# Windowed attention and eight experts: slot table from plain one-hots, copies of v a step later, and the second expert's weights on another queue

## The chip, the cores and the metric

The kernel runs on one core of a Trainium2 chip. The core has five engines that run side by side, each with a queue of its own: TensorE (PE: matmuls; the loading of a matmul's stationary operand is listed apart as PEld), VectorE (DVE), ScalarE (ACT), GpSimd (POOL) and SyncE (SP), which here only issues DMA transfers. DMAs are also issued from ScalarE's queue and, with row numbers computed in the kernel, from GpSimd's. The metric is the time of one execution on the device in microseconds. The kernel before took 696.98 us, the median of 3 runs (695.01 to 697.22).

## The reference

Two layers. The first is attention with 8 batches, 8 heads, 576 positions and 64 dimensions; every query sees itself and the 63 keys before it. The second sends each of the 8 x 576 = 4608 tokens (512 numbers each) to one of 8 experts, the one with the largest gate logit, and scales what the expert gives by the gate's probability.

```python
scores = scale * np.matmul(q, k.transpose(0, 1, 3, 2))
mask = (rel >= 0) & (rel < window)          # window = 64
...
attn = attn / (np.sum(attn, axis=-1, keepdims=True) + 1e-09)
return np.matmul(attn, v).astype(np.float32)
...
x = np.ascontiguousarray(attn_out.transpose(0, 2, 1, 3)).reshape(B * S, H * D)
...
logits = x @ w_gate
expert_idx = np.argmax(logits, axis=1)
gate_w = probs[np.arange(N), expert_idx]
perm = np.argsort(expert_idx, kind='stable')
...
    h = np.maximum(x_sorted[lo:hi] @ w1[e], 0.0)      # 512 -> 1024
    y_sorted[lo:hi] = h @ w2[e]                        # 1024 -> 512
return (gate_w[:, None] * y).astype(np.float32)
```

## The kernel before

**Attention.** The work is cut into 16 units (`units`): a batch group of two batches (`bg`, four of them) and a pair of heads (`g`, four of them). A unit has 9 token tiles of 128 tokens, and is worked in three steps of three tiles, so there are 48 steps. One call of `step(s)` issues parts of several steps: the scores of step s+1 (`scored`, L700), their masking and row maximum on VectorE (`masked`, L713), the exponential on ScalarE (`softened`, L723), the turning of step s's probabilities on TensorE with a copy out (`flipped`, L731 and L733), the product of step s-1 with v (`weighted`, L746) and its division (`divided`, L756 to L760), which writes x into a tile of the pool `xsp` (seven tiles, three to a batch group), and the turning of x for the gate's logits (`x_turned`, L771, and `logit`, L783).

The order on each engine is the order in which the code issues (`tc.manual_schedule()`). Two dictionaries, `todo` and `between`, name for each step what is to be issued at its end or in its middle. At every third step, that is once a unit, `load_v(u + 2)` and `load_qk(u + 3)` are issued. v is kept twice, as loaded (`va`) and shifted by half a tile (`vb`); `load_v` issues four DMAs on SP's queue and six GpSimd copies that make `vb` (L638 to L646).

**Routing.** When a batch group's logits are complete (`ripe`), `choose(bg)` finds on VectorE each token's expert and its rank among that expert's tokens. `after` spreads this over the next steps, and with it `weigh` (x times the gate, on GpSimd at L886), `store` (x to DRAM) and `place(j)`. A token's slot is a number; its low part (0 to 127) says the lane, its high part which of 62 columns. `place(j)` writes for token tile j two 128x128 matrices `lo[:, 0, j]` and `lo[:, 1, j]` (L875): the one-hot of the low part, times one of two parts of the token's number (`toks`, from L196 to L199). `slot_table` makes the one-hot of the high part, `hi` (L919), for all 36 token tiles, and multiplies the two for 36 x 2 matmuls that sum into `slots` (`fill`, L927); L937 makes of it the list of token numbers by slot, `perm_i`. `first_tiles` does the same earlier for the first two tiles of expert 0, from the first 27 token tiles alone: `hi_e` has 4 columns, 27 x 2 matmuls at L990, `perm_e` at L993, then `gather_first`.

**Experts.** Tokens are worked in tiles of 256 (two chunks of 128). `hidden(e)` makes the first layer and `output(e)` the second; both use seven products of half-size blocks in place of eight, with sums of weight blocks prepared on GpSimd (`sums_w1`, `sums_w2`, L142) and sums of data on VectorE. `hidden` is a generator of seven parts and `output` of eight, so that the code can issue other work between them: the first tile (`tile0`) is issued in parts among the last batch group's routing, `starts` and the eight parts of `slot_table`. The x of a later tile comes by an indirect DMA (`gather`, L283 and L285), is turned on VectorE in 16 blocks (`turned_blocks`, L324), copied on ScalarE to its place (`keep_turned`, L336) and put into sums (`sums_x`, L342). `some(blocks, n)` issues n of these transposes: in `hidden` 6, 2, 2 and 2 after four of its adds, and `output` issues those that are left. For the second tile, `tile1`, `hidden(0)` is called without blocks, so all 16 are issued in `output`. The result of a tile goes out by `scatter` (L304).

**Memory and weights.** There are two sets of weight buffers. Set 0 exists from the start; set 1 is taken from a pool `wp` that is opened behind the block of the attention and the first two tiles, in memory that pools of that block (`held`) had. Its first loads, w1 and w2 of expert 1, 2 MB each, are issued on SP's queue.

Of the kernel before, what the change touches and what calls it, by code (L numbers as in the profile page):

```python
# [36 lines left out]
def kernel(  # L37
# [130 lines left out]
    lo = consts.tile([P, 2, NJ, P], BF16, name="lo")  # L168
    count = consts.tile([P, E], F32, name="count")
    lane = consts.tile([P, P], BF16, name="lane")  # L170
    low = consts.tile([P, NJ], F32, name="low")
    hi_id = consts.tile([P, NS], BF16, name="hi_id")

    toks = [consts.tile([P, NJ], F32, name=f"tok_{n}") for n in "ab"]
# [5 lines left out]
    with tc.tile_pool(name="tmp", bufs=1) as tmp:  # L180
        iota(e_m[:], pattern=[[1, E]], base=-E, channel_multiplier=0)
        ids = tmp.tile([P, P], F32, name="ids")
        iota(ids[:], pattern=[[1, P]], base=0, channel_multiplier=0)
        V.tensor_copy(out=lane[:], in_=ids[:])
        V.tensor_scalar_add(hi_id[:], ids[:, 0:NS], float(-C))

        tok = tmp.tile([P, NJ], F32, name="tok")
        tok_g = tok[:].rearrange("p (g j) -> p g j", j=NTB)
        for i in range(BG):
            iota(tok_g[:, :, i * NV : (i + 1) * NV], pattern=[[BG * S, NJ // NTB], [P, NV]], base=i * S,  # L190
                 channel_multiplier=1)
            iota(tok_g[i * D : (i + 1) * D, :, BG * NV], pattern=[[BG * S, NJ // NTB]], base=i * S + SM,
                 channel_multiplier=1)
        tok_i = tmp.tile([P, NJ], I32, name="tok_i")
        low_i = tmp.tile([P, NJ], I32, name="low_i")
        V.tensor_scalar(out=tok_i[:], in0=tok[:], scalar1=-1.0, scalar2=float(NT), op0=ALU.mult, op1=ALU.add)  # L196
        V.tensor_single_scalar(low_i[:], tok_i[:], D - 1, op=ALU.bitwise_and)
        V.tensor_copy(out=toks[1][:], in_=low_i[:])
        V.tensor_tensor(out=toks[0][:], in0=tok_i[:], in1=low_i[:], op=ALU.subtract)  # L199
        G.memset(ones[:], 1.0)  # L200
        G.affine_select(
            out=before[:], in_=ones[:], pattern=[[1, P]], compare_op=ALU.is_gt, fill=0.0, base=0,
            channel_multiplier=-1,
        )
        G.memset(keep[:], 1.0)
        G.memset(keep[:, :, 0:1], 0.0)
        V.memset(count[:], 0.0)
# [7 lines left out]
    hi_e = rt.tile([P, NJE, NE * C], BF16, name="hi_e")  # L215
# [129 lines left out]
    def hidden(e, blocks=iter(())):  # L345
# [18 lines left out]
        some(blocks, 6)  # L364
# [6 lines left out]
        some(blocks, 2)  # L371
# [3 lines left out]
        some(blocks, 2)  # L375
# [4 lines left out]
        some(blocks, 2)  # L380
# [186 lines left out]
    with tc.manual_schedule(), ExitStack() as held, ExitStack() as brief:  # L567
        xsp = held.enter_context(tc.tile_pool(name="xsp", bufs=7))
# [63 lines left out]
        def load_v(u, batches=range(BG)):  # L632
            bg, g = units[u]
            va, vb = v_ring[u % NVR]
            for i in batches:
                for h in range(2):
                    nc.sync.dma_start(out=va[:, i, :, h, 0:D], in_=whole(v, u, i, h))
                nc.gpsimd.tensor_copy(  # L638
                    out=vb[0:D, i].rearrange("p j h d -> p (j h d)"),
                    in_=va[D:P, i].rearrange("p j h d -> p (j h d)"),  # L640
                )
                nc.gpsimd.tensor_copy(
                    out=vb[D:P, i, 0 : NV - 1].rearrange("p j h d -> p (j h d)"),
                    in_=va[0:D, i, 1:NV].rearrange("p j h d -> p (j h d)"),
                )
                G.tensor_copy(out=vb[D:P, i, NV - 1, :, 0:D], in_=rests[bg][2][D:P, i, 2 * g : 2 * g + 2])  # L646
# [226 lines left out]
        def place(j):  # L873
            for i in range(2):
                V.tensor_scalar(  # L875
                    out=lo[:, i, j], in0=lane[:], scalar1=low[:, j : j + 1], scalar2=toks[i][:, j : j + 1],
                    op0=ALU.is_equal, op1=ALU.mult,
                )
# [29 lines left out]
        def slot_table(hi):  # L908
# [8 lines left out]
            for n in range(2):  # L917
                js = slice(n * NJ // 2, (n + 1) * NJ // 2)
                V.tensor_tensor(  # L919
                    out=hi[:, js], in0=_inner(at_b[:, js], NS), in1=_ins(hi_id[:], 1, NJ // 2), op=ALU.is_equal  # L920
                )
                yield
            slots = banks[3](0, NS)

            def fill(j):
                for i in range(2):
                    nc.tensor.matmul(slots, lhsT=lo[:, i, j], rhs=hi[:, j], start=(i + j == 0), stop=(i + j == NJ))  # L927

            for j in range(NJE):
                fill(j)  # L930
            for n in range(NST):
                for m in range(ST):
                    place(NJE + n * ST + m)
                yield
            for j in range(NJE, NJ):
                fill(j)
            V.tensor_scalar(out=perm_i[:], in0=slots, scalar1=-1.0, scalar2=float(NT), op0=ALU.mult, op1=ALU.add)  # L937
# [13 lines left out]
        def after(s, routing, bg):  # L951
# [3 lines left out]
            if bg < last - 1:  # L955
# [3 lines left out]
                for m in range(NTB):  # L959
                    do(5 + m * 2 // 3, partial(place, bg * NTB + m))  # L960
                    do(5 + m * 2 // 3, partial(weigh, bg, m, G))
                    if m % ST == ST - 1:
                        do(5 + m * 2 // 3, partial(store, bg, m // ST, G))
# [4 lines left out]
            for m in range(NTB):  # L968
                do(4 + m // 3, partial(place, bg * NTB + m))
# [7 lines left out]
        def first_tiles():  # L977
# [5 lines left out]
                out=hi_e[:], in0=_inner(key[:], NE * C), in1=_ins(hi_id[:, C + 1 : C + 1 + NE * C], 1, NJE),  # L983
                op=ALU.is_equal,
            )
            yield
            slots = banks[next(tr_ring)](0, NE * C)
            for j in range(NJE):
                for i in range(2):
                    nc.tensor.matmul(  # L990
                        slots, lhsT=lo[:, i, j], rhs=hi_e[:, j], start=(i + j == 0), stop=(i + j == NJE)
                    )
            V.tensor_scalar(out=perm_e[:], in0=slots, scalar1=-1.0, scalar2=float(NT), op0=ALU.mult, op1=ALU.add)  # L993
# [4 lines left out]
        V.memset(lo[:, 0, 0:4], 0.0)  # L998
        for _ in range(8):
            nc.tensor.matmul(  # L1000
                banks[7](0, 512), lhsT=lo[:, 0, 0], rhs=lo[:, 0, 0:4].rearrange("p a b -> p (a b)"), start=True,
# [10 lines left out]
        load_v(1)  # L1012
        load_qk(2)
# [12 lines left out]
        def step(s):  # L1026
# [11 lines left out]
            if s >= 0 and s % NST == 0:  # L1038
# [3 lines left out]
                if u + 2 < NU:  # L1042
                    load_v(u + 2)
                if u + 3 < NU:
# [70 lines left out]
        hi = held.enter_context(tc.tile_pool(name="hot", bufs=1)).tile([P, NJ, NS], BF16, name="hi")  # L1115
# [10 lines left out]
        tile1 = chain(hidden(0), output(0, blocks))  # L1126
        for _ in range(8):
            next(tile1)
        regs, end, most = loads()
# [4 lines left out]
    wp = ctx.enter_context(tc.tile_pool(name="wp", bufs=1))  # L1134

    w1s.append(w1_of(wp, 1))
    s1s.append(s1_of(wp, 1))
    w2s.append(w2_of(wp, 1))
    s2s.append(s2_of(wp, 1))


    with tc.manual_schedule():
        load_w1(1)
        load_w2(1)
# [116 lines left out]
```

## Time and profile before

| | |
|---|---|
| runs | 696.98 us median (695.01 to 697.22, 3 runs) |
| the profiled execution | 692.44 us, its span from first to last instruction 690.7 us |
| granted TensorE clock | 0.997 of full speed |
| attention and routing | about 0 to 199 us |
| first tile, with the slot table | about 200 to 231.8 us |
| second tile | 231.8 to 257 us |
| experts 0 (rest) to 7 | 257 us to the end |

All times of instructions are from that one execution, in microseconds from its start. A row of the order of time reads: start, duration of the group, engine, line, operation, what it writes <- what it reads, size, count, and in brackets how long the engine stood idle before it and what ended that. A row of a line's instructions gives the shortest, median and longest duration in ns. Matmuls overlap one another, so a group of them lasts longer than the distance to the next group's start; that distance is the pace. Busy shares are averages over stages with different limits.

### The profile page before, as it was taken

The numbers are of one execution on the slowest core, as the hardware profiler recorded it, in microseconds if no ns is written. First come the engines' busy times: TensorE is split into PE (matmuls) and PEld (weight loads), VectorE is DVE, ScalarE is ACT, GpSimd is POOL, SyncE is SP. The second block draws the span as 40 slices with busy tenths as digits, with TensorE's granted clock in tenths as the row PEclk, the third lists the DMA queues.
The fourth block names the chain that finished last, engine by engine and source line by source line (L and its number), as shares of the span: only waits on it lengthen the run. The fifth ranks groups of instructions, "written<-read, shape, count | busy, mean of one in ns | idle before, by whom it ended". The sixth has DMA issues, their size and how long they took to land. (4 is left out here: it accounts for less than half of the span.)

```text
span 690.7 us, 17952 instructions
## 1 busy us (share of the span) xinstructions
PE 671.8 (97%) x6902; PEld 590.5 (85%) x6902; DVE 500.6 (72%) x1650; ACT 262.2 (38%) x660; POOL 357.0 (52%) x364
## 2 busy tenths in 40 slices
PE   7999999999999999999999999999899999999996
PEld 5888888888788987998899899899599799689995
DVE  5767898898959578775686586577767586866864
ACT  4989888889845011211121121111121121121211
POOL 7316578577771218676451446446265756264012
PEclk9999999999999999999999999999999999999998
DMA  9999888877524442723601171270145171211012
GB/s 216 251 210 199 192 206 244 202 199 198 162 78 168 155 157 77 268 69 128 230 1 64 61 262 44 70 269 32 65 156 190 51 256 51 65 39 63 2 63 61
DMA packets 135742, 94.51 MB, mean 137 GB/s; under 512 B 114543, under 2 KB 114559, under 8 KB 135616
## 3 DMA queue, kind: packets, MB, share of 16 engines
q1 hardware_dynamic: 113952, 38.28, 22.4%
q0 software_dynamic: 8544, 26.50, 11.9%
q10 hardware_dynamic: 13120, 28.05, 11.3%
q8 instruction: 78, 1.28, 0.7%
q14 instruction: 48, 0.39, 0.2%
HBM read 73.94 MB, written 20.45 MB: 137 GB/s over the span
## 5 line engine op out<-in xcount | busy, mean ns | idle before, releaser
L324 DVE STREAM_TRANSPOSE v_m<-qk_m 32x256 f32<-32x256 f32 x320 | 139.3, 435 | 6.8 <-DMA qk_m<-x_dram,at_g 0.8
L285 POOL DMA_INDIRECT qk_m<-x_dram,at_g x42 | 45.1, 1075 | 164.2 <-DVE v_m L324 154.1
L353 PE MATMUL bank<-qk_m,s 128*128 128x128 f32 x1024 | 122.5, 275 | 0.0
L353 PEld LDWEIGHTS bank<-qk_m,s 128*128 128x128 f32 x1024 | 118.3, 192 | 0.0
L723 ACT ACTIVATE pr<-pr,mx 128x128 f32<-128x128 f32 x288 | 89.6, 391 | 22.2 <-DVE mx L713 21.7
L353 PE MATMUL bank<-qk_m,w 128*128 128x128 f32 x768 | 94.2, 276 | 1.0 <-PEq L1166 0.6
L353 PEld LDWEIGHTS bank<-qk_m,w 128*128 128x128 f32 x768 | 90.3, 192 | 4.6 <-issue 4.3
L713 DVE CUSTOM_DVE_ANT_0 pr<-bank,mask 128x128 f32<-128x128 f32 x288 | 64.4, 286 | 15.8 <-PE bank L700 14.6
L304 POOL DMA_INDIRECT out_dram<-v_m,at_s x42 | 42.5, 1011 | 56.9 <-DVE v_m L393 52.7
L393 DVE TENSOR_TENSOR v_m<-bank,v_m 128x256 f32<-128x256 f32 (+1 forms) x95 | 43.8, 480 | 38.1 <-PE bank L397 27.3
L142 POOL TENSOR_TENSOR s<-w 128x1024 f32<-128x1024 f32 x22 | 52.2, 2374 | 0.0
L638 POOL COPY v_m<-v_m 64x520 f32<-64x520 f32 x32 | 19.8, 618 | 62.1 <-DMA v_m<-in_v_dram 52.8
L397 PE MATMUL bank<-qkT_m,v_m 128*128 128x256 f32 x216 | 48.3, 379 | 0.0
L746 PEld LDWEIGHTS bank<-v_m,pT 128*64 128x64 f32 x1152 | 40.4, 137 | 9.0 <-issue 3.4
L746 PE MATMUL bank<-v_m,pT 128*64 128x65 f32 x1152 | 47.4, 227 | 0.1
L360 ACT COPY qk_m<-bank 128x512 f32<-128x512 f32 x16 | 9.4, 587 | 99.9 <-PE bank L353 73.7
L336 ACT COPY qk_m<-v_m 128x512 f32<-128x512 f32 x40 | 22.7, 615 | 61.4 <-DVE v_m L324 61.4
L397 PEld LDWEIGHTS bank<-qkT_m,v_m 128*128 128x128 f32 x216 | 41.0, 190 | 5.5
L700 PE MATMUL bank<-qkT_m 64*64 64x128 f32 x1152 | 43.1, 278 | 1.6 <-DVE qkT_m L670 1.6
L886 POOL TENSOR_SCALAR xs<-xs,gate 128x512 f32<-128x512 f32 x27 | 42.2, 1574 | 0.9 <-DVE gate L846 0.3
L731 PE MATMUL bank<-ident,pr 128*128 128x128 f32 x288 | 42.0, 282 | 0.0
L363 DVE TENSOR_TENSOR qk_m<-bank,qk_m 128x512 f32<-128x512 f32 x16 | 11.1, 692 | 40.7 <-PE bank L353 40.7
(202 smaller groups left out, 1249.2 us busy)
## 6 DMA issues: line engine op xcount, KB each, us to landing
w<-in_moe_w_dram ACTq DMA_DIRECT2D x9, 2048.0 KB, 8.1
qk_m<-in_q_dram SPq DMA_DIRECT2D x32, 256.0 KB, 5.1
v_m<-in_v_dram SPq DMA_DIRECT2D x64, 128.0 KB, 4.3
qk_m<-in_k_dram SPq DMA_DIRECT2D x30, 256.0 KB, 5.1
qk_m<-in_moe_w_dram ACTq DMA_DIRECT2D x3, 2048.0 KB, 10.6
w<-in_moe_w_dram SPq DMA_DIRECT2D x2, 2048.0 KB, 14.2
w<-in_moe_w_dram ACTq DMA_DIRECT2D x4, 512.0 KB, 5.8
x_dram<-xs POOLq DMA_DIRECT2D x4, 512.0 KB, 5.6
```

What stands on the lines that cost most here:

```text
L142: op()
L285: G.indirect_dma_start(out=xg[c], out_offset=None, in_=x_dram[:, :], in_offset=bass.IndirectOffsetOnAxis(ap=at_g[:, c : c + 1], axis=0),)
L304: put = G.indirect_dma_start(out=out[:, :], out_offset=bass.IndirectOffsetOnAxis(ap=at_s[:, c : c + 1], axis=0), in_=ys[c], in_offset=None ...
L324: V.transpose(out=xn[b * QD : (b + 1) * QD, :, :, a * QD : (a + 1) * QD].rearrange("p c g i -> p (c g) i"), in_=rows[a * QD : (a + 1) * QD ...
L353: nc.tensor.matmul(acc[:, f, :], lhsT=a[:, g, f * P : (f + 1) * P], rhs=b[:, g, :], start=(first and f == 0 and g == 0), stop=(g == HG - 1 ...
L393: plus = lambda out, a, b: V.tensor_tensor(out=out, in0=a, in1=b, op=ALU.add)
L397: nc.tensor.matmul(acc, lhsT=a[:, f, :], rhs=b[:, f, :], start=(start and f == 0), stop=(stop and f == HF - 1), skip_group_check=True,)
L700: nc.tensor.matmul(out_, lhsT=qT[rows, t, a * WINDOW : (a + 1) * WINDOW], rhs=rhs, start=True, stop=True, skip_group_check=True,)
L713: V.tensor_tensor_reduce(out=prs[h][:, m, :], in0=scs[h][:, m, :], in1=mask[:, m0 + m, :], scale=-scale, scalar=-2 * MASKED, op0=ALU.add, ...
L723: nc.scalar.activation(out=y, in_=y, func=AF.Exp, scale=-1.0, bias=mx[:, h, m : m + 1])
L746: nc.tensor.matmul(px[a * D : (a + 1) * D, h, m, :], lhsT=pTs[h][:, m, a * D : (a + 1) * D], rhs=vt[:, h, :], start=True, stop=True, skip_ ...
L886: engine.tensor_scalar(out=y, in0=y, scalar1=s, scalar2=None, op0=ALU.mult)
```

## The change

It has these parts:

- `lo` holds one matrix for each token tile, the plain one-hot of the low part; `place(j)` makes three tiles with one compare, so it is called for every third tile only. `low` is kept in bf16.
- The token's number is split as before in two parts, but multiplied on the side of `hi`: `with_tokens` makes two more planes of `hi`, one with a GpSimd product by `tok_a` and one with a ScalarE copy scaled by `tok_b` (one number a partition, since the low six bits are the same in each tile). `hi` and `hi_e` have three planes.
- `table_of` does one matmul for each token tile with both planes as moving operand (2 x 62 columns, or 2 x 4), and sums the two halves with two VectorE operations. In `slot_table` all 36 come at the end.
- `load_v` only loads; the GpSimd copies, `copy_v`, are issued at the head of the next step's list.
- `xsp` has eight tiles.
- `held` is closed and `wp` opened before the second tile; expert 1's w1 and w2 are loaded on ScalarE's queue, after the third and the fifth part of that tile. Its 16 transposes are shared out as 0, 4, 4 and 4 in `hidden`, and the last four in `output`.

```diff
-    lo = consts.tile([P, 2, NJ, P], BF16, name="lo")
+    lo = consts.tile([P, NJ, P], BF16, name="lo")
-    low = consts.tile([P, NJ], F32, name="low")
+    low = consts.tile([P, NJ], BF16, name="low")
-    toks = [consts.tile([P, NJ], F32, name=f"tok_{n}") for n in "ab"]
+    tok_a = consts.tile([P, NJ], F32, name="tok_a")
+    tok_b = consts.tile([P, 1], F32, name="tok_b")
...
-        V.tensor_scalar(out=tok_i[:], in0=tok[:], scalar1=-1.0, scalar2=float(NT), op0=ALU.mult, op1=ALU.add)
+        V.tensor_copy(out=tok_i[:], in_=tok[:])
         V.tensor_single_scalar(low_i[:], tok_i[:], D - 1, op=ALU.bitwise_and)
-        V.tensor_copy(out=toks[1][:], in_=low_i[:])
-        V.tensor_tensor(out=toks[0][:], in0=tok_i[:], in1=low_i[:], op=ALU.subtract)
+        V.tensor_copy(out=tok_b[:], in_=low_i[:, 0:1])
+        V.tensor_tensor(out=tok_a[:], in0=tok_i[:], in1=low_i[:], op=ALU.subtract)
+        V.tensor_scalar_add(tok_a[:], tok_a[:], -float(NT))
...
-    def hidden(e, blocks=iter(())):
+    def hidden(e, blocks=iter(()), shares=(6, 2, 2, 2)):
...
-        some(blocks, 6)
+        some(blocks, shares[0])
...
-        xsp = held.enter_context(tc.tile_pool(name="xsp", bufs=7))
+        xsp = held.enter_context(tc.tile_pool(name="xsp", bufs=8))
...
-        def load_v(u, batches=range(BG)):
+        def load_v(u):
+            bg, g = units[u]
+            va = v_ring[u % NVR][0]
+            for i in range(BG):
+                for h in range(2):
+                    nc.sync.dma_start(out=va[:, i, :, h, 0:D], in_=whole(v, u, i, h))
+        def copy_v(u):
             bg, g = units[u]
             va, vb = v_ring[u % NVR]
-            for i in batches:
-                for h in range(2):
-                    nc.sync.dma_start(out=va[:, i, :, h, 0:D], in_=whole(v, u, i, h))
+            for i in range(BG):
                 nc.gpsimd.tensor_copy(
...
         def place(j):
-            for i in range(2):
-                V.tensor_scalar(
-                    out=lo[:, i, j], in0=lane[:], scalar1=low[:, j : j + 1], scalar2=toks[i][:, j : j + 1],
-                    op0=ALU.is_equal, op1=ALU.mult,
-                )
+            js = slice(j, j + ST)
+            V.tensor_tensor(out=lo[:, js], in0=_inner(low[:, js], P), in1=_ins(lane[:], 1, ST), op=ALU.is_equal)
+
+        def with_tokens(hi, js):
+
+            n, ns = js.stop - js.start, hi.shape[3]
+            G.tensor_tensor(out=hi[:, 1, js], in0=hi[:, 0, js], in1=_inner(tok_a[:, js], ns), op=ALU.mult)
+            nc.scalar.activation(
+                out=hi[:, 2, js].rearrange("p j s -> p (j s)"), in_=hi[:, 0, js].rearrange("p j s -> p (j s)"),
+                func=AF.Copy, scale=tok_b[:],
+            )
+
+        def table_of(perm, hi, n, bank, first):
+
+            slots = bank(0, 2, hi.shape[3])
+            for j in range(n):
+                nc.tensor.matmul(slots, lhsT=lo[:, j], rhs=hi[:, 1:, j], start=(j == 0), stop=(j == n - 1))
+            V.tensor_scalar_add(first, slots[:, 0], float(NT))
+            V.tensor_tensor(out=perm, in0=slots[:, 1], in1=first, op=ALU.add)
...
+                with_tokens(hi, js)
                 yield
-            slots = banks[3](0, NS)
...
-            for j in range(NJE):
-                fill(j)
             for n in range(NST):
-                for m in range(ST):
-                    place(NJE + n * ST + m)
+                place(NJE + n * ST)
                 yield
-            for j in range(NJE, NJ):
-                fill(j)
-            V.tensor_scalar(out=perm_i[:], in0=slots, scalar1=-1.0, scalar2=float(NT), op0=ALU.mult, op1=ALU.add)
+            table_of(perm_i[:], hi, NJ, banks[3], first_s[:])
...
+            with_tokens(hi_e, slice(0, NJE))
             yield
...
+            table_of(perm_e[:], hi_e, NJE, banks[next(tr_ring)], first_e[:])
             gather_first(perm_e[:, 0:C])
...
                     load_v(u + 2)
+                    todo.setdefault(s + 1, []).insert(0, partial(copy_v, u + 2))
...
         blocks = turned_blocks()
-        tile1 = chain(hidden(0), output(0, blocks))
-        for _ in range(8):
+        held.close()
+        wp = ctx.enter_context(tc.tile_pool(name="wp", bufs=1))
+        w1s.append(w1_of(wp, 1))
...
+        tile1 = chain(hidden(0, blocks, (0, 4, 4, 4)), output(0, blocks))
+        for n in range(8):
             next(tile1)
+            if n in (2, 4):
+                (load_w1 if n == 2 else load_w2)(1, nc.scalar)
...
-        load_w1(1)
-        load_w2(1)
```

## The prediction

> **What bounds the kernel now.** I read the busy shares first, then the order of time on TensorE (PE) around the places that the diff touches, and then what VectorE (DVE), GpSimd (POOL) and the queues do in those stretches. The page's first part, and the row of the operation that the change replaces:
>
> ```profile
> PE 671.8 (97%) x6902; PEld 590.5 (85%) x6902; DVE 500.6 (72%) x1650; ACT 262.2 (38%) x660; POOL 357.0 (52%) x364
> L875 DVE TENSOR_SCALAR lo<-lane,low,tok_a x36: 301/309/735, 91.9 to 231.0; 128x128 bf16<-128x128 bf16 x36
> ```
>
> PE is the bound nearly everywhere. An edit pays only where it takes PE instructions away or fills a PE gap. After 258 us the diff changes no instruction, and PE's order is full there, so what is won before is carried to the end. The row's longest instance, 735 ns against 309, will matter below.
>
> Order of time on PE at the slot table, then at the first table and the first gather:
>
> ```profile
> 221.73 1.89 PE L397 MATMUL bank<-qkT_m,v_m 128*128 128x256 f32 x8
> 223.91 1.22 PE L927 MATMUL bank<-hi,lo 128*128 128x62 bf16 x36 [0.30 <-DVE qk_m L342]
> 225.47 0.68 PE L927 MATMUL bank<-hi,lo 128*128 128x62 bf16 x18 [0.33 <-DVE hi L919]
> 225.99 3.70 PE L397 MATMUL bank<-qkT_m,v_m 128*128 128x256 f32 x16
> 229.52 1.89 PE L397 MATMUL bank<-qk_m,v_m 128*128 128x256 f32 x8
> 231.25 0.69 PE L927 MATMUL bank<-hi,lo 128*128 128x62 bf16 x18
> 231.77 2.03 PE L353 MATMUL bank<-qk_m,w 128*128 128x128 f32 x16
> ...
> 191.43 1.50 PE L990 MATMUL bank<-hi_e,lo 128*128 128x4 bf16 x54
> 199.17 0.66 PE L315 MATMUL bank<-ident,qk_m 128*128 128x128 f32 x4 [0.28 <-DMA qk_m<-x_dram,perm_e]
> ```
>
> A group's duration holds the tail of its last matmul; the pace is the distance of starts. Eight L397 take 1.73 us (225.99 to 229.52 for sixteen, 229.52 to 231.25 for eight). Eighteen L927 take 231.77 - 231.25 = 0.52 us, 28.9 ns each. Fifty-four L990 take 1.35 us to the next row at 192.78, 25 ns each.
>
> **Slot table.** Removed: 72 matmuls of 62 columns, and the two stops ahead of them. From the end of the product at 221.73 (223.46 by its pace) to the next tile's start at 231.77 PE takes 8.31 us. Afterwards it has three products (3 x 1.73 = 5.19) and then 36 matmuls of 124 columns in one piece. Twice the columns at the same pace per column is 57.8 ns each, 2.08 us. Sum 7.27: a gain of **1.0 us**. A rule speaks against it. The Trainium skill (TensorE: Matmul & The Clock Gate, section Back-to-back issue gap) gives about 81 ns per matmul for streams of weight load and matmul at 128 columns, and 128/2.4 + 2.5 = 56 ns for the isolated gap. By 81 ns the table costs 2.92 us and the gain is 0.1; the trace's pace at 62 columns (28.9 ns) is that of the isolated form, so I keep 57.8.
>
> What has to be ready at 223.46 + 5.19 = 228.65: the three last one-hots and both token products. DVE writes the halves of hi at 221.41 and 224.10 (1.3 us each, as now). POOL then multiplies 18 x 62 = 1116 elements per half. No such POOL operation stands in the trace; nearest is the two-input row
>
> ```profile
> L142 POOL TENSOR_TENSOR s<-w 128x1024 f32<-128x1024 f32 x22 | 52.2, 2374 | 0.0
> ```
>
> 2.32 ns an element: 2.6 us a half. Half one runs 222.8 to 225.4, half two 225.5 to 228.1, 0.5 us early. With the one-input weighing of L886 as the price (1559 ns for 512, 3.0 ns an element) the second ends at 229.6 and PE stands for 1 us. I take 2.6 and keep 0 to 1 us for the range. ScalarE's copy with a scale is hidden: it is idle from 219.85 to 233.9, and 1116 elements cost about 1.1 us by its 512-element copies of 587 ns (under 1.3 us even in proportion). Each place of three tiles becomes one tensor-tensor of 384 elements. Nearest is L760's 558 ns for 384 (0.47 to the next start) in place of six starts 0.223 us apart, 1.34 us. The one-hots are then ready near 227.9. Two DVE operations in place of one write perm_i (223 ns now), 0.2 us more; they delay only the gather, which still leaves about 0.8 us sooner than its 233.25.
>
> **First table.** 27 matmuls for 54, at the 25 ns issue pace: 0.67 us less. The work before it gets shorter by 1.34 - 0.47 = 0.87 us on DVE (place at 189.55), so the small POOL product (108 elements, about 0.4 us with its start) fits between hi_e, then near 190.45, and PE's arrival at 191.2. It is queued ahead of the memset of L292, which now runs about 191 to 192, behind it the gather. The gather waits for perm_e (193.03 + 0.16 now). With DVE's scores of the next step also earlier and 0.2 us for the second operation, perm_e comes about 0.55 us sooner. PE meets the landed rows at 199.17 after a 0.28 us wait, so the gain here is bounded by the gather: **0.6 us** (0 if the POOL product is late, 0.95 if the wait goes too).
>
> **Places in the attention.** The steps' scores L700 start 3.72 or 3.85 us apart where nothing stands in the way. Steps that hold two tiles' places are longer: 91.26 to 95.45 is 4.19, 137.52 to 141.51 is 3.99, 152.83 to 157.01 is 4.18, 1.2 us over 3.72 in all; in the first, places until 93.1 push L713, the exponentials and the copy that PE's L771 then waits for. One 0.47 us operation replaces 0.89 us per such step. The Trainium skill (GPSIMD Engine Reference, section Specifications) has a rule against this too: POOL shares its SBUF interfaces with VectorE, with contention for instructions of two SBUF inputs, which the new compare is. The row above shows up to 735 ns beside L886 on POOL with the old form as well. If each of the six moved compares lost the worst 0.43 us, the gain would vanish; if none does, it is 1.2. I take **0.8**.
>
> **v copied a step later, eighth x slot.** POOL waits 52.8 us for v in all at L638; it has no direct PE waiter. The copies for unit u+2 are needed about six steps later (22 us), and POOL's largest backlog is nine weighings, 14 us. The loads on SP keep their order; behind the copies stand only weighings and POOL's stores. L760 shows no listed wait for a slot. Both: 0, between -0.3 and +0.3. The startup's one more DVE operation (about 0.2 us) lies before 7.31, where DVE has been idle for 3.69.
>
> **The tile after the table.** The 16 transposes (7.17 us at 248.49, 0.448 each) move: four after each of three adds in the hidden stage, four left. The ScalarE copy after them then comes about 3.4 us earlier, and PE's one stop goes:
>
> ```profile
> 256.98 8.93 PE L453 MATMUL bank<-qk_m,w 128*128 128x160 f32 x64 [0.36 <-ACT qk_m L336]
> 242.99 0.19 POOL L283 COPY at_g<-perm_i 128x2 int32<-128x2 int32 x1 [4.65 <-DMA qk_m<-x_dram,at_g]
> 231.97 0.38 SPq L159 DMA_DIRECT2D w<-in_moe_w_dram  x1
> ```
>
> **0.35 us.** What takes its place (clock of before): the add at 239.20 ends 239.8, four transposes to 241.6, the next add to 242.2; PE's second accumulation into that bank starts 242.57. The left sums end 249.25 for a product at 249.54. Both fit by 0.3 us, so the bound is a loss of 0.3. Expert 1's two 2 MB loads leave SP at 232 and go onto ScalarE's queue after its relus, about 238 and 243. Each holds ScalarE 0.38 us with the next relu 3 us away. On SP nothing stands behind them. The memory that they fill is free once the table's matmuls have read hi (231.9 now, sooner then); the x stores left SP at 219 and took 3 us. They land by about 255 (18 us the slowest now); POOL first reads w1 at 262.77.
>
> **Sum.** 1.0 + 0.6 + 0.8 + 0.35 = 2.75 us. The profiled execution took 692.44 (span 690.7, 1.74 around it): 689.7. It lies 4.5 under the median of the runs, 696.98; the same saving off the median gives **694.2 us**. A measurement of this kernel tells about 0.3%, 2.1 us, from no change.
>
> **Rivals.**
> (A) The gain is eaten: matmuls at 81 ns (0.9 lost), or POOL at 3 ns an element (1 lost), and port waits in the attention (0.8 lost): about 0.9 left, 696.1. For it: the bounds above; against it: the rows. Chance 0.17, within 0.3%.
> (B) Slower: the gather that follows the table (for the tile behind this one) lands late. The row at 242.99 shows its second half, issued 234.56, landing only then, 8.4 us later, as the first weight load ended (10.4 us from 231.97); alone a gather lands in 3.8. DVE now meets it at 239.9, not 248.5. In the new order it is issued about 233.6 and the loads at 236.8, with packets some 1.5 us after. If it has not landed by then it may land with w1, near 246.5 on the old clock: DVE stands 6.6 us in order, PE with it in the bank's second accumulation, and 6.6 - 2.4 is 4.2 slower: 701.2. It decides at a landing past 239.9, and the whole turns slower past 242.3. About one microsecond of margin: chance 0.14, 0.13 of it above 0.3%.
> (C) More: 164.88 to 182.50 holds 2.9 us beyond the step's pace, where routing on DVE runs beside nine weighings. If POOL's freer order and the lighter DVE take two thirds of that, 692.2. Against it: those weighings wait for the gate, not for v. Chance 0.11.
>
> **How the numbers follow.** The main case has 0.58, itself from 692.8 to 696.0 by the ends kept above; 0.43 of it is over 2.1 us, 0.15 within. Faster 0.43 + 0.11 = 0.54; within 0.15 + 0.17 + 0.01 = 0.33; slower 0.13. The range 691.5 to 698.0 holds the main case, A and most of C and leaves B out.
>
> **What would show it.** Right: PE's L927 successor in one run of 36 at about 58 ns straight after a product, no stop ahead; next tile about 1 us closer to 221.73; no stop at L453; PE's first L315 without a longer DMA wait. Wrong: PE stopped for POOL ahead of the table; spacing near 80 ns; DVE's transposes waiting for the gather in the hidden stage; L700 distances at places unchanged.

## The result, and the profile after

The changed kernel takes 690.51 us (median of 11 runs, 688.72 to 692.71) against 695.3 us of the kernel before in the same comparison (11 runs, 692.4 to 697.51). The ratio is 0.9941, with an interval of 0.992 to 0.9961: 2.7 to 5.6 us less. Its profiled execution took 690.51 us, span 688.8 us, granted clock 0.998.

The page's first part, after:

```profile
PE 668.8 (97%) x6839; PEld 589.1 (86%) x6839; DVE 489.3 (71%) x1593; ACT 265.5 (39%) x663; POOL 361.7 (53%) x367
```

The line of the new compare after (shortest, median and longest in ns):

```profile
L883 DVE TENSOR_TENSOR lo<-low,lane x12: 545/548/1097, 96.3 to 231.7; 128x384 bf16<-128x384 bf16 x12
```

PE has 63 matmuls and as many weight loads fewer (6902 to 6839): 36 at the slot table, 27 at the first table. That number matters again below. The compare's usual 548 ns is the neighbour's 558 of the forecast; its worst instance takes twice as long.

The order of time on PE after, at the first table, the slot table and the second tile:

```profile
194.72 0.83 PE L898 MATMUL bank<-hi_e,lo 128*128 128x8 bf16 x27
...
224.52 5.34 PE L401 MATMUL bank<-qkT_m,v_m 128*128 128x256 f32 x24
229.70 1.89 PE L401 MATMUL bank<-qk_m,v_m 128*128 128x256 f32 x8
231.42 2.13 PE L898 MATMUL bank<-hi,lo 128*128 128x124 bf16 x36
233.39 2.00 PE L357 MATMUL bank<-qk_m,w 128*128 128x128 f32 x16
...
250.09 1.99 PE L401 MATMUL bank<-qk_m 128*128 128x256 f32 x8 [0.48 <-ACT v_m L415]
...
258.83 8.86 PE L457 MATMUL bank<-qk_m,w 128*128 128x160 f32 x64
```

The slot table is one run of 36, straight behind a product: 233.39 - 231.42 = 1.97 us, 54.7 ns each. From the product that began at 221.73 before (224.52 here) to the next tile's start it takes 8.87 us where it took 10.04. The stop ahead of L457 is gone, but there is a new one of 0.48 us inside the second tile, at 250.09.

Cutting the whole span at PE's landmarks, with the kernel before profiled twice (us):

| stage | before | before again | after |
|---|---|---|---|
| start to the ninth step's scores | 36.06 | 36.42 | 41.21 |
| attention, to the last scores | 153.14 | 155.59 | 151.48 |
| last scores to the first tile (first table) | 11.29 | 11.25 | 10.57 |
| first tile with the slot table | 31.28 | 31.29 | 30.13 |
| second tile | 25.21 | 25.21 | 25.44 |
| the rest, from 257 us on | 433.72 | 435.24 | 429.97 |
| span | 690.7 | 695.0 | 688.8 |

Two rows were not in the forecast and are larger than its whole sum: the start is 5 us longer, and the part behind 257 us, where the diff touches nothing, is 4 to 5 us shorter. The attention varies by more than 2 us between executions of one kernel.

### The profile page after: what moved, and what is told of

The parts are those of the page before. It is cut to its first block, busy times and chain, and to the rows that moved or that the text cites. A ratio compares the mean times of both kernels' runs of the same rounds, so it can differ in the third digit from the quotient of the medians.

```text
span 688.8 us, 17762 instructions
## 1 busy us (share of the span) xinstructions
PE 668.8 (97%) x6839; PEld 589.1 (86%) x6839; DVE 489.3 (71%) x1593; ACT 265.5 (39%) x663; POOL 361.7 (53%) x367
```

## The experiments

**Which part gives what.** Three kernels do one part each, and one is the kernel before once more. `onehots` takes only the one-hots (in outline):

```diff
-    lo = consts.tile([P, 2, NJ, P], BF16, name="lo")
+    lo = consts.tile([P, NJ, P], BF16, name="lo")
...
+            table_of(perm_i[:], hi, NJ, banks[3], first_s[:])
...
+            table_of(perm_e[:], hi_e, NJE, banks[next(tr_ring)], first_e[:])
```

> The kernel before with the one-hots, the token planes and the two tables of the change alone; v's copies, seven x slots, the second tile and expert 1's loads as before. Theory (the tables and the places carry the gain, as predicted): 2.4 to 2.8 us faster, ratio about 0.996; L700-like score steps at two-tile places back to 3.72, the start of the second tile 2.5 us closer to the step at 36 us. Rival (the gain lies in the second tile and behind it): ratio within 0.001 of 1.

Measured: 691.35 us against 694.36, ratio 0.9964 (0.9939 to 0.9989). Start 39.96, first table 10.47, first tile 30.12, the rest 429.89. The ratio is the one expected, but by luck: it holds a start that is 3.9 us longer and a rest that is 3.8 us shorter, and the expectation had neither.

`tile1` takes only the second tile's part:

```diff
+        held.close()
+        wp = ctx.enter_context(tc.tile_pool(name="wp", bufs=1))
-        tile1 = chain(hidden(0), output(0, blocks))
+        tile1 = chain(hidden(0, blocks, (0, 4, 4, 4)), output(0, blocks))
...
+            if n in (2, 4):
+                (load_w1 if n == 2 else load_w2)(1, nc.scalar)
```

> The kernel before with the second tile's part alone: pools closed early, expert 1's weights on ScalarE's queue, transposes shared out as 0, 4, 4, 4. Theory: the stop of 0.36 us goes and one of 0.48 us at the third product of the output comes (a copy queued behind a delayed relu), so 0 to 0.3 us slower, ratio 1.000. Rival (the early issue of the loads frees the queues for what comes behind 258 us, where the two profiles differ by 3.7 us): ratio 0.995, and the PE stops named issue in the rest tiles are gone.

Measured: 695.92 us against 694.36, ratio 1.0019 (1.0002 to 1.0037). The second tile takes 25.31 for 25.21; the rest, 435.16, is that of before.

`cv` only loads v and copies it a step later:

```diff
+                    todo.setdefault(s + 1, []).insert(0, partial(copy_v, u + 2))
```

> The kernel before with v's copies a step later alone (seven x slots). Theory: no direct PE waiter, ratio within 0.001 of 1. Rival (POOL's copies no longer delay VectorE's routing steps): the score distance of 4.28 us at 71.7 to 76.0 falls to 3.85 in each of three routings, 0.4 to 1.3 us faster, ratio 0.998 to 0.999.

Measured: 693.18 us against 694.36, ratio 0.9992 (0.9977 to 1.0007). Start 35.75, the rest 435.38.

`before_again` has no edit.

> The kernel before, unchanged, profiled once more. Theory (the start and the rest tiles' stops vary from one execution to the next): the ninth score step's start and the length of the two rest tiles' first stage differ from the first profile (36.06; 7.45 and 6.41 us) by a microsecond or more. Rival (they belong to the code): within 0.3 us of them.

Measured: 696.85 us, one run; its stages stand in the table above. The start (36.42) and the first stages of the rest tiles (7.48 and 6.23) are within 0.4 us of the first profile: they belong to the code and do not come and go. What follows: both surprises, the long start and the short rest, come with the one-hots, and neither with the other two parts.

**The start: an address.** With `lo` and `low` smaller, what is allocated behind them slides: `qk_m`, which takes q and k, began at byte 73984 of a partition, a multiple of 256, and begins at 64576, 64 bytes past one; `v_m` moved from 133376 to 123968 likewise. The loads of q, k and v write rows of 256 bytes. In `v_m` these rows lie 65 numbers, 260 bytes, apart (`VW`), so that nearly all of them are off a multiple of 256 in both kernels; the rows that the slide takes off it are those in `qk_m`. Two stretches of 5 us of the start, before (busy time of PE, PEld, DVE, ACT and POOL, then the granted clock, the DMA share and GB/s; the share is the time of all packets over that of 16 engines, and passes 1 where packets overlap):

```profile
5.00:10.00 5.00, 4.12 (x43) 3.38 (x42) 1.50 (x8) 1.05 (x3) 4.74 (x10) 1.00 1.28 288
15.00:20.00 5.00, 4.92 (x89) 4.18 (x90) 3.75 (x25) 4.82 (x15) 2.95 (x7) 1.00 0.81 183
```

The same stretches after:

```profile
5.00:10.00 5.00, 3.82 (x41) 2.91 (x40) 1.23 (x6) 0.79 (x2) 4.71 (x10) 1.00 1.40 204
15.00:20.00 5.00, 2.92 (x54) 2.14 (x46) 2.05 (x15) 3.48 (x10) 2.83 (x6) 1.00 1.33 208
```

Between 5 and 10 us the packets take more time (1.40 for 1.28) and move less (204 GB/s for 288). PE then gets 54 matmuls done between 15 and 20 us where it did 89. `aligned` is the changed kernel with 192 bytes ahead of `qk_m`, which puts it at 64768, again a multiple of 256:

```diff
+    consts.tile([P, 48], F32, name="pad")
```

> The changed kernel with 192 bytes of padding ahead of qk_m, so that qk_m and v_m start at a multiple of 256 bytes in SBUF as they do in the kernel before (in the changed kernel they start 64 bytes past one). Theory (the slower start comes from loads of 256-byte rows that straddle such a boundary): the DMA rate at 5 to 10 us is back from 204 to 288 GB/s, the ninth score step starts near 36 us, not 41, and the time is 4 to 5 us below the changed kernel's, ratio to the kernel before about 0.988. Rival (the slower start comes from the order of v's copies or from chance): start near 40 to 41 us, ratio 0.994. If the shorter experts' stage (430 us, not 434 to 435) came from the addresses too, it is lost here.

Measured: 684.94 us against 692.15, ratio 0.9884 (0.9857 to 0.9911). Start 36.13; the same stretch in this kernel:

```profile
5.00:10.00 5.00, 4.12 (x44) 3.30 (x42) 1.62 (x10) 1.19 (x4) 4.71 (x10) 1.00 1.28 285
```

`before_off` is the kernel before with 320 bytes ahead of `qk_m` (now 74304, 64 past a multiple of 256), and nothing else:

```diff
+    consts.tile([P, 80], F32, name="pad")
```

> The kernel before with 320 bytes of padding ahead of qk_m, so that qk_m and v_m start 64 bytes past a multiple of 256 (of 512 too), nothing else. Theory (alignment alone makes the slow start): ninth score step at 40 to 41 us in place of 36, 204 GB/s at 5 to 10 us, ratio about 1.006; the experts' stage stays at 434 to 435 us. Rival: unchanged, ratio 1.000; or, if the addresses carry the experts' gain, that stage falls to 430 us.

Measured: 697.03 us against 692.15, ratio 1.0069 (1.0044 to 1.0095); start 40.19, and 195 GB/s between 5 and 10 us. So the address alone costs the kernel before 3.1 to 6.6 us, and giving it back to the changed kernel removes its long start. The cause of the start is shown in both directions. The padding moves every tile behind it, so that `qk_m` rather than a tile behind it is to blame is read from the layout, not tested alone.

**The rest: the place of PE's instructions.** From 257 us on the kernel works the same tiles. The difference lies mostly in the two rest tiles (`rest_tile`, a smaller tile for an expert's last tokens, entered by a branch). PE's order in their first stage, 48 matmuls, in the kernel before:

```profile
491.07 1.93 PE L500 MATMUL bank<-w,qk_m 128*32 128x256 f32 x30
494.39 4.20 PE L500 MATMUL bank<-w,qk_m 128*32 128x256 f32 x18 [1.39 <-issue]
...
597.25 2.94 PE L500 MATMUL bank<-w,qk_m 128*32 128x256 f32 x35 [0.20 <-issue]
600.51 3.22 PE L500 MATMUL bank<-w,qk_m 128*64 128x512 f32 x13 [0.32 <-issue]
```

and after:

```profile
596.70 5.52 PE L504 MATMUL bank<-w,qk_m 128*32 128x256 f32 x48
602.15 0.44 PE L517 MATMUL bank<-ident,qk_m 128*128 128x128 f32 x2
```

Before, PE stands between the 30th and the 31st of 48 matmuls, and in the other tile behind the 35th, with nothing that it waits for ("issue"). This first stage took 7.45 and 6.41 us; after, it takes 5.45 in both. The whole rest tiles took 14.29 and 13.24 us and take 12.29 each, that is 3.0 us; in the second profile of the kernel before they took 15.89 and 13.06, with two more such stops in the tile's second stage, 4.4 us. In the mean of all profiles 3.9 of the 4.7 us lie in these two tiles; the remainder isn't placed. `dummies` gives the changed kernel its 126 PE instructions (63 matmuls with their weight loads) back, as unused work at the start:

```diff
+        for _ in range(63):
+            nc.tensor.matmul(banks[7](0, 4), lhsT=lo[:, 0], rhs=lo[:, 0, 0:4], start=True, stop=True, skip_group_check=True)
         load_qk(0)
```

> The changed kernel with 63 added matmuls of 4 columns behind the warm-up, whose results nobody uses, so that TensorE has as many instructions ahead of the experts as in the kernel before. Theory (the experts' gain of 4 to 5 us is a matter of where TensorE's instructions lie when a rest tile is branched to): the first stage of the two rest tiles goes from 5.45 back to about 7.5 and 6.2 us and the experts' stage from 430 to about 434 us; ratio to the kernel before about 0.999 to 1.001. Rival (the gain comes from the data: addresses or the loads' order): 5.45 and 430 us stay, ratio 0.994 to 0.997.

Measured: 696.25 us against 692.15, ratio 1.005 (1.0031 to 1.0069). First stages 7.21 and 6.39, the rest 433.58, with the stops again behind the 30th and the 35th matmul. The ratio is above the 0.999 to 1.001 expected; at the 25 ns of a short matmul the 63 cost some 1.6 us themselves (an estimate), the remainder isn't placed. `dum16` and `dum32` put 16 and 32 such matmuls into `aligned`:

> The padded kernel with 16 unused matmuls of 4 columns behind the warm-up (32 instructions more on TensorE). Theory A (the stop depends on where a branch target lies within a block that is fetched): the two rest tiles' first stages change, to anything from 5.45 to 8 us, each in its own way. Theory B (only the number of instructions counts, with a limit): 5.45 and 5.45 stay, the experts' stage stays at 430 us.

> The padded kernel with 32 unused matmuls of 4 columns behind the warm-up (64 instructions more on TensorE). Theory A (position within a fetched block): lengths of 5.45 to 8 us that need not lie between those with 16 and with 63. Theory B (the number, with a limit): 5.45 or, past the limit, about 7.2 and 6.4 us in both, as with 63.

Measured: 686.52 and 686.78 us (one run each, before 693.52); first stages 5.45 throughout, the rest 430.27 and 429.95. So it is not each added instruction that costs. Number or place was still open: `dum48` and `dum75` shift the place by 15 matmuls one way and 12 the other against 63, and `late63` has the 63 behind the last expert, where they lengthen the program and shift nothing:

```diff
                 expert(e)
+            for _ in range(63):
+                nc.tensor.matmul(banks[7](0, 4), lhsT=mask[:, 0], rhs=mask[:, 0, 0:4], start=True, stop=True, skip_group_check=True)
             finish()
```

> The aligned kernel with 48 unused matmuls of 4 columns (96 PE instructions) ahead of the first load; it computes the same. Place theory (a PE stop sits at a fixed place in the instruction stream, so that it moves by one matmul for each one added in front): the stop that stood behind the 30th matmul of the first rest tile before, and with 63 added, now stands behind the 45th of its 48, with about 1 to 1.4 us; the second rest tile's stop (behind the 35th) would be behind the 50th, so outside these 48: its stage takes 5.45. First stage of the rest tiles 6.6 to 7.2 and 5.45. Number theory (a program with more than some number of PE instructions stops there): either 5.45 and 5.45, or 7.2 and 6.4 with the stops behind the 30th and 35th.

> The aligned kernel with 75 unused matmuls (150 PE instructions) ahead of the first load; it computes the same. Place theory: the stops stand behind the 18th of the 48 matmuls in the first rest tile and behind the 23rd in the second. Number theory: behind the 30th and the 35th as before, 7.2 and 6.4 us.

> The aligned kernel with 63 unused matmuls (126 PE instructions) behind the last expert's last product, so that the program has as many PE instructions as the kernel before while every instruction up to there stands where it stands in the aligned kernel; it computes the same. Place theory: first stage of the rest tiles 5.45 and 5.45 us, no stop inside them. Number theory: 7.2 and 6.4 us with stops behind the 30th and 35th matmul. The span grows by the unused matmuls' own 2 to 4 us at the end.

Measured: first stages 5.45 and 5.45 in `dum48`, 7.42 and 7.22 in `dum75`, 5.45 and 5.45 in `late63`; one run each, 685.41, 691.14 and 686.36 us beside 696.58. The order on PE in `dum75`:

```profile
489.15 1.48 PE L505 MATMUL bank<-w,qk_m 128*32 128x256 f32 x18
491.99 4.65 PE L505 MATMUL bank<-w,qk_m 128*32 128x256 f32 x30 [1.36 <-issue]
...
595.15 1.93 PE L505 MATMUL bank<-w,qk_m 128*32 128x256 f32 x30
598.24 4.20 PE L505 MATMUL bank<-w,qk_m 128*32 128x256 f32 x18 [1.16 <-issue]
```

`late63` settles that the program's length isn't it: as many instructions as before, no stop. In the first rest tile the stop moved from behind the 30th to behind the 18th with 12 matmuls more in front, one for one: a fixed place in PE's stream. Two forecasts of that theory failed. `dum48` should have stopped behind the 45th and did not, and in the second tile the stop went from 35 to 30, not to 23. For the first there is a reading from the rows: whatever the place, the next instructions come about 3 us after the tile's first matmul (494.39 - 491.07 = 3.32, 600.51 - 597.25 = 3.26, here 2.84 and 3.09), and without a stop PE gets past the 45th only 4.5 us after it, so it would find them there.

The traces show where they come from. Among the DMA queues of the page before is

```profile
q8 instruction: 78, 1.28, 0.7%
```

(packets, MB, share of the DMA engines' time): 78 packets of 16 KB. They keep step with PE: between 15.0 and 192.6 us of that profile PE starts 253 matmuls and weight loads for each. Seven profiles have the stops in both tiles (`before`, `before_again`, `before_off`, `cv`, `tile1`, `dummies` and `dum75`). In each of the 14 stops one such packet lands after the tile has begun, and PE goes on 1.2 to 1.6 us after it has landed: before, the packets land at 492.94 and 599.16, and PE goes on at 494.39 and 600.51. In `dum48` the packet lands at 488.38, 1.8 us after the tile's first matmul, with time to spare for the 45th. So PE runs out of instructions behind the branch and waits for the next block of them. This rests on the times of the packets and the stops; no edit moved a packet alone. Why the place in the second tile goes from 35 to 30 stays open.

**The loads, and GpSimd's margin.** `early` issues expert 1's two loads on ScalarE's queue ahead of the second tile, so that the gather for the next tile runs beside them (rival B of the forecast, forced):

```diff
+        load_w1(1, nc.scalar)
+        load_w2(1, nc.scalar)
         tile1 = chain(hidden(0, blocks, (0, 4, 4, 4)), output(0, blocks))
         for n in range(8):
             next(tile1)
-            if n in (2, 4):
-                (load_w1 if n == 2 else load_w2)(1, nc.scalar)
```

> The changed kernel with expert 1's two weight loads issued on ScalarE's queue ahead of the second tile, not after its third and fifth part. Theory of the prediction's rival B: the gather lands with the first weights, some 8 us after its second half was issued, VectorE's first transposes wait for it, and the second tile takes 25.4 + 3 to 7 us. Rival (a gather keeps its pace beside the loads): 25.4 us unchanged.

Measured: one run, 694.43 us; the second tile takes 29.18 for 25.44. VectorE in its order of time in this kernel:

```profile
244.58 1.78 DVE L328 STREAM_TRANSPOSE v_m<-qk_m 32x256 f32<-32x256 f32 x4 [3.20 <-DMA qk_m<-x_dram,at_g]
```

and PE:

```profile
247.14 3.39 PE L357 MATMUL bank<-qk_m,s 128*128 128x128 f32 x16 [2.92 <-DVE qk_m L378]
```

VectorE waits for the gather, and PE for VectorE. In the change itself GpSimd's copy that follows the landing stands at 240.81, not at 244.52 as here: rival B is real, and did not happen. `pool_twice` is `aligned` with GpSimd's product of `hi` issued twice:

```diff
+            G.tensor_tensor(out=hi[:, 1, js], in0=hi[:, 0, js], in1=_inner(tok_a[:, js], ns), op=ALU.mult)
```

> The padded kernel with each of GpSimd's two token products issued twice in a row (the second writes the same values). Theory (the product hides by 0.1 us only): PE stands 2 to 4 us ahead of the 36 matmuls, the first tile takes 32 to 34 us where it took 30.12, and the first table loses about 0.4 us. Rival (cover to spare): under 1 us.

Measured: one run, 688.21 us; the first tile takes 33.89 for 30.12. The first table takes 10.81, where `aligned` took 10.65: 0.2 us lost, and 0.4 expected. PE now stops inside the slot table:

```profile
224.55 1.15 PE L900 MATMUL bank<-hi,lo 128*128 128x124 bf16 x18
228.68 1.81 PE L900 MATMUL bank<-hi,lo 128*128 128x124 bf16 x18 [2.99 <-POOL hi L890]
```

In the change as it stands GpSimd's second product runs from 229.01 for 2.31 us, to 231.32, and PE is at the table at 231.42. A tenth of a microsecond of cover is all there is.

**A faster version.** `best` is `aligned` with two of the transposes moved from the last share to the output:

```diff
-        tile1 = chain(hidden(0, blocks, (0, 4, 4, 4)), output(0, blocks))
+        tile1 = chain(hidden(0, blocks, (0, 4, 4, 2)), output(0, blocks))
```

> The changed kernel with qk_m aligned (192 bytes of padding) and the second tile's transposes shared out as 0, 4, 4, 2 and six left, so that the copy of the first output product (ScalarE, queued behind the last relu) comes 0.9 us sooner. Theory: PE's stop of 0.48 us ahead of the third product of the output is gone, the second tile takes 24.8 to 25.0 us where the padded kernel took 25.3, the ratio to the kernel before is 0.987 to 0.988. Rival (the six left make the next tile's copy late): a stop at the half tile, second tile 25.3 or more.

Measured: 684.13 us against 693.52, ratio 0.9862 (0.983 to 0.9895), the second tile 24.67, a little better than expected. It beats both kernels.

## Why the prediction was wrong, step by step

The forecast was 694.2 us with a range down to 691.5; 690.51 lies under it, 3.7 us from the forecast. Of these, 1.7 us are the base: the kernel before measured 696.98 over three runs and 695.3 over eleven. The saving of 2.75 us lies at the edge of the measured 2.7 to 5.6, but it isn't what happened: three terms that the forecast put at nothing measured -4.7, +4.5 and -1.3 us, -1.5 together. With means over all profiled kernels that share a feature (us; minus is a gain):

| term | predicted | measured | from |
|---|---|---|---|
| slot table | -1.0 | -1.15 | first tile 31.3 to 30.1, in all |
| first table | -0.6 | -0.7 | 11.25 to 10.55 |
| places in the attention | -0.8 | about -0.55 | steps 23, 35 and 39 |
| v copied later | 0 | about -1.3 | step 18, 5.2 to 3.9 |
| second tile | -0.35 | +0.1 to +0.2 | 25.21 to 25.3, 25.44 |
| start | 0 | +4.5 | 36.2 to 40.7, `dum75` (38.49) left out |
| behind 257 us | 0 | -4.7 | 434.7 (old tables) to 430.05 (new, no stops) |

The sum, about -3.7, lies within the measured interval. Without the start's term it is -8.2, and `aligned` measured 0.9884 of 692.15, -8.0. The start's term alone is +4.5, and `before_off` measured +4.8.

**Slot table: right; first table: right in size.** At the slot table the choice between 57.8 and 81 ns a matmul was decided by the trace's own pace, and 54.7 came out. The Trainium skill's rule of a sustained gap (TensorE: Matmul & The Clock Gate, section Back-to-back issue gap) would have made 2.92 us of it; 1.97 were measured, and the isolated form's 56 ns is the one that fits here. (By 81 ns the forecast's own sum leaves a gain of 8.31 - 5.19 - 2.92 = 0.2 us, not 0.1.) GpSimd's product took 2.05 and 2.31 us where 2.6 were taken, but it began later than forecast: VectorE's second half of `hi`, beside it, took 2.04 us instead of 1.3:

```profile
224.21 1.32 DVE L941 TENSOR_TENSOR hi<-at_b,hi_id 128x1116 bf16<-128x1116 bf16 x1
226.90 2.04 DVE L941 TENSOR_TENSOR hi<-at_b,hi_id 128x1116 bf16<-128x1116 bf16 x1
```

The 0.5 us of slack became 0.1. "The one-hots are then ready near 227.9" was too early as well: the last two took 1.56 us together beside GpSimd, and ended at 232.2, behind PE's arrival at 231.42. PE met each one in time, because it reads the tiles in order. At the first table the 27 matmuls take 0.69 us (194.72 to 195.41) where 54 took 1.35. The gather, named there as the bound, did not decide in this profile: PE no longer waits for its rows, but 0.65 us for a copy of VectorE at 200.38.

**Places in the attention: half.** Step 39 gains what was said (4.10 to 3.72 in the mean), step 23 half of it (4.24 to 3.97), and step 35 gets a little longer (4.06 to 4.15), each by the mean of the profiles. Rival A's port waits are there, but not at the compares: in `dum32` the compare of step 39 lasts 1.00 us beside GpSimd, and the step is still 3.72. In step 35 after, the compare keeps its 0.55 us, and PE waits for the division ahead of it. Ahead of that division, two small operations of the routing, 0.17 us each elsewhere, last until GpSimd's copies of v end (139.35 and 139.90):

```profile
138.75 0.63 DVE L878 TENSOR_SCALAR r_half<-r_pos 128x9 int32<-128x9 int32 x1
139.41 0.51 DVE L879 CAST low<-r_half 128x9 bf16<-128x9 int32 x1
...
142.59 0.97 PE L754 MATMUL bank<-v_m,pT 128*64 128x65 f32 x24 [0.39 <-DVE xs L768]
```

How much of the missing gain such waits took isn't shown.

**v copied later: put at nothing, and a gain.** The step said of GpSimd's wait for v that "it has no direct PE waiter". It looked only at who waits for the copies, not at what GpSimd does in their place in time. In `before_again`, routing on VectorE meets a weight sum of GpSimd:

```profile
72.09 2.37 POOL L1053 TENSOR_TENSOR s<-w,s 128x1024 f32<-128x1024 f32 x1
72.32 2.23 DVE L819 TENSOR_TENSOR r_top<-r_top,e_m 128x72 f32<-128x72 f32 x1
76.65 0.55 PE L771 MATMUL bank<-ident,xs 128*128 128x128 f32 x3 [1.89 <-DVE pT L733]
```

An operation of 0.23 us takes 2.23 us: it ends when GpSimd is done (74.46), and PE loses 1.89 us. In `cv` the copies are out of the way, so that the last sum runs from 65.66 and is over before the routing begins at 70.4:

```profile
65.66 2.37 POOL L1060 TENSOR_TENSOR s<-w,s 128x1024 f32<-128x1024 f32 x1
...
70.44 0.23 DVE L819 TENSOR_REDUCE r_mx<-logits 128x9 f32<-128x72 f32 x1
```

Step 18 took 5.8 us in three of the five profiles of kernels that copy v at once and 4.1 to 4.3 in the others, and 3.8 to 4.1 in all that copy later. Each of the three has such an operation, of 2.2 to 2.3 us, in this step, and no other profile has one. That `cv` alone measured within its interval of no change is in keeping with 1.3 us (its interval reaches to 1.6). The rule on shared interfaces that the forecast weighed (the Trainium skill, GPSIMD Engine Reference, section Specifications) fits these rows. The worst wait that the forecast read from the trace for it, 0.43 us, was not the worst: here it was 2.00 us, nearly the whole GpSimd operation.

**Second tile: the term was reversed.** The old stop went, as forecast. "What takes its place" was checked for the adds and for the left sums, but not for ScalarE's order. ScalarE's copy of the output's first product before, and the same with what stands ahead of it after:

```profile
246.34 0.37 ACT L411 COPY v_m<-bank 128x256 f32<-128x256 f32 x1 [0.43 <-PE bank L397]
...
249.15 0.63 ACT L389 ACTIVATE qk_m<-qk_m 128x512 f32<-128x512 f32 x1 [1.91 <-DVE qk_m L388]
249.68 0.35 ACT L415 COPY v_m<-bank 128x256 f32<-128x256 f32 x1
```

Before, the copy waited for PE alone. After, the last relu waits for VectorE, whose last add now stands behind the transposes; the copy of the output's first product is queued behind that relu, and PE's third product into its bank waits for the copy: the 0.48 us at 250.09. `best` moves two transposes out of the last share; its copy runs at 242.50 and PE has no stop, 0.6 us better than `aligned`.

**"After 258 us the diff changes no instruction, and PE's order is full there, so what is won before is carried to the end": the step that failed.** It put this stage at nothing, and the stage gained 4.7 us. No instruction changes, but their place in PE's stream does, and PE's order was not full: the stops named "issue" stood in the trace of before, where the first stages of the two rest tiles took 7.45 and 6.41 us and not 5.45. They were passed over because no engine was named as their cause.

**The start: not in the sum at all.** The forecast looked at what the startup computes, and not at where in memory the tiles end up when one of them shrinks: +4.5 us.

**The rivals.** A did not happen as told: the matmuls kept 54.7 ns, GpSimd took 2.05 and 2.31 us, and the gain that the attention lacks was not lost at the compares, where A had the port waits. B did not happen. C's routing stretch did not gain (17.62 us before, 17.61 after); what gained was one routing step beside GpSimd's sums. The two errors of nearly 5 us, of opposite sign, hid each other: that the saving came near the forecast's is luck.

## What to carry to other kernels

When a tile in SBUF changes its size, look up where the tiles behind it begin: here 64 bytes cost 4.5 us of the start, and 192 bytes of padding bought them back. A stop named "issue" on the engine that bounds the kernel can be won or lost by an edit that only changes the number of instructions ahead of it; look at the packets of the instruction queue there, and say what the stop costs before saying that a later stage is untouched. When work on GpSimd moves, look at which operation of VectorE it will then run beside, and, when work is put ahead of an operation, at everything queued behind that operation on each engine.

## What the runs showed of the hardware

- Between 5 and 10 us, while rows of 256 bytes are loaded, the core's DMA moved 195 to 204 GB/s in the five kernels whose `qk_m` begins 64 bytes past a multiple of 256 in SBUF, and 278 to 288 in the twelve where it begins at a multiple. The Trainium skill (DMA: Bandwidth & Descriptors, section How a descriptor splits into AXI transactions) says that a transaction that reads begins at a 256-byte boundary and that a descriptor off it takes extra beats; here the side that is written was moved, and the loss, 29% from 288 to 204, was measured on it.
- A VectorE operation can take longer beside a GpSimd operation by about what is left of the latter. With two SBUF inputs on each: 2.23 us for 0.23 with 2.14 left, 2.04 for 1.32 with 0.85 left, 1.10 for 0.55 with 0.68 left. With one on each: 0.63 for 0.17 with 0.60 left.
- PE can stop inside a straight run of matmuls behind a branch, until 1.2 to 1.6 us after a 16 KB packet of the instruction queue has landed; the stage of 5.45 us then took 6.1 to 7.8. The place moves with the number of instructions in front: in the first rest tile behind the 30th matmul with 63 more than in the changed kernel, behind the 18th with 75 more, nowhere in the stage with 0, 16, 32 or 48 more.
